# A chain of attention, MoE and routed MoE on one core: low parts earlier in VectorE's queue, two low halves later, one pair of routing dots per step

## Chip, cores and metric

One core of a Trainium2 chip. The metric is the device time of one execution in microseconds. Names used below: TensorE (PE in rows, PEld for its weight loads), VectorE (DVE), ScalarE (ACT), GpSimd (POOL), SyncE (SP), which issues the transfers.

## What is computed

Three parts in a chain, all in float32 (sizes: 8 sequences of 3072 tokens, 256 columns; z has 64).

```python
scores = (1.0 / S) * np.matmul(z, z.transpose(0, 2, 1))
x = u * np.matmul(np.maximum(scores, 0.0) ** 2, v)          # attention
h = x @ w_in                                                # MoE-1, 256 -> 2048
x = (h * (1.0 / (1.0 + np.exp(-h)))) @ w_out
e_idx = np.argmax(x @ w_gate, axis=1)                       # routed MoE-2, 8 experts
for e in range(E):
    mask = e_idx == e
    h = np.maximum(x[mask] @ w1[e], 0.0)
    out[mask] = gate_w[mask, None] * eom[mask, e, None] * (h @ w2[e])
```

## The kernel before

**Splitting.** A float32 product is made of three products of a narrower type: every operand is split into a high part (ScalarE's copy to fp32r, now and then VectorE's CAST at L296) and a low part, what the high part leaves, which is a subtraction on VectorE (L269 in attention, L355 in MoE-1, L690 in MoE-2). TensorE computes high x high, high x low, low x high.

**Items and steps.** The program is one list of items, each with a front and a back. An attention item is one tile of 128 keys against 512 queries: its front makes the scores (two matmuls, L288 and L289, then ReLU and square on ScalarE), its back the product with v (six matmuls of 512 columns, L312 to L314). Scores are symmetric: a tile whose mirror image has been computed is not computed again, it is fetched from memory (`sym`, L241, four transfers issued by SyncE into a staged tile `raw`) and transposed by VectorE (L249, "flip"). A tile on the diagonal is partly fetched. Such a mirrored step has no score matmuls. A MoE-1 item is 128 of the 2048 hidden columns for a block of 512 tokens: front six matmuls (L346), sigmoid on ScalarE (L348), the product g of the two on VectorE (L350), high part on ScalarE (L353); back twelve matmuls of 256 columns (L380 to L382). MoE-2 items are alike.

There are 48 blocks of 512 tokens. The first five blocks' attention items stand alone in the list (24 each); from there attention and MoE-1 items of earlier blocks alternate, then MoE-1 items alone, then MoE-2. Item i's front is in step i, its low part in step i+1, its back in step i+3 (`LOOK`). The names below give a step its number from 0.

**The order.** A scheduler is not at work: each engine executes its instructions in the order in which the program is written, and the loop at the end of `moe_chain` (L953 on) writes it. In each step: `run_tasks(i, 0.0)` writes the tasks whose due step has come; then the front of item i; then the low part of item i-1 (`rest`); then the back of item i-3; then `run_tasks` again with a budget, which takes tasks that are released but not yet due, in the order of their due steps, until their costs have used the budget up. The budget comes from the item whose back it is: 1.1 for most MoE-1 items, 0.8 for attention items that compute scores, 0 for mirrored ones, 1.4 for MoE-2.

**Tasks.** Loads of z, x, v and mirrored scores go through a ring of four `raw` tiles (`DEPTH`); the task of a tile (`f_prep`) works on it and then issues the load of the tile four places later. For z that work is `prep_hl` (the high half by ScalarE, the low half of the lower 64 rows by VectorE, L170), for x it is `f_x` (L209, L210), for mirrored scores the transpose L249. Routing of a finished MoE-1 block is `route_tasks`: 32 dot products on VectorE (`dot`, L390; four rows of tokens by eight experts), two to a task, here a pair; then `pick` (L423 to L437, small operations on VectorE), then, four steps later, `rank` with two small matmuls and the scattered stores by GpSimd. All are released when the block is done and due at the end of the next block. `later(steps, cost, fn, slack)` puts a task a few steps ahead. At block 46 `snapshot` counts the tokens per expert (a matmul at L397 on the running one-hot counts `ohc` that `pick` updates) and makes the table of tiles for MoE-2.

Of the kernel before, what the change touches and what calls it, by code (L numbers as in the profile page):

```python
# [14 lines left out]
ALU = mybir.AluOpType  # L15
AX = mybir.AxisListType

P = 128
# [6 lines left out]
LEAD = 5  # L25
# [10 lines left out]
def r32(ap):  # L36
    return ap.bitcast(F32)
# [7 lines left out]
def moe_chain(tc, zT, uT, vp, win, wout, w12, wgT, wogT, out):  # L45
    nc = tc.nc
    B, NQ, DZ, _ = zT.shape
# [4 lines left out]
    KT = S // P  # L52
# [17 lines left out]
    with ExitStack() as ctx:  # L70
# [13 lines left out]
        def mk(pool, shape, dt, tag, bufs):  # L84
            uid[0] += 1
            return pool.tile(shape, dt, tag=tag, name=f"{tag}_{uid[0]}", bufs=bufs)

        def psum():
            return mk(pp, [P, TQ], F32, "ps", 4)
# [55 lines left out]
        def task(due, release, cost, fn):  # L145
            tasks.append((due, release, len(tasks), cost, fn))

        items = []
        now = [0]

        def later(steps, cost, fn, slack=2):
            i = now[0] + steps
            bisect.insort(queue, (i + slack, i, len(tasks), cost, fn))
            tasks.append(None)
# [3 lines left out]
        hl = [ap_.tile([P, TQ], F32R, name=f"hl{j}") for j in range(NHL)]  # L158
# [8 lines left out]

        def prep_hl(j, zz):
            nc.scalar.activation(hl[j], zz, AF.Copy)
            nc.vector.tensor_tensor(out=hl[j][DZ:P], in0=zz[DZ:P], in1=r32(hl[j][DZ:P]), op=ALU.subtract)  # L170

        def prep_hh(zz):
            h = mk(ap_, [P, TQ], F32R, "hh", 2)
# [26 lines left out]
        def f_x(n, c):  # L200
            def f(t):
                if c == 0:
                    if n == NBLK - 1:
                        h, l = (mk(cp, [P, ND, TQ], F32R, g, 1) for g in ("xf", "x"))
                    else:
                        h, l = (mk(ap_ if g == "xo" else cp, [P, ND, TQ], F32R, g, 1) for g in (("xo", "x") if n % 2 else ("xh", "xl")))
                    xs[n] = [h[:, i, :] for i in range(ND)], [l[:, i, :] for i in range(ND)]
                h, l = xs[n]
                nc.scalar.activation(h[c], t, AF.Copy)  # L209
                nc.vector.tensor_tensor(out=l[c], in0=t, in1=r32(h[c]), op=ALU.subtract)  # L210
            return f


# [10 lines left out]
        def key_order(b, q):  # L224
            if not any(columns(b, q, k) for k in range(KT)):
                return list(range(KT))
            own = range(q * NS, (q + 1) * NS)
            lead = [k for k in range(KT) if k // NS == q + 1]
            o = lead + [k for k in range(KT) if k not in lead and k not in own]
            for s, k in enumerate(own):  # L230
                o.insert(s * KT // NS, k)
            return o
# [152 lines left out]
        def small(shape, dt, tag, bufs=2):  # L385
            return mk(cp, shape, dt, tag, bufs)

        def dot(a, w, res):
            j = mk(cp, [P, TQ], F32, "junk", 1)[:, 0:D]
            nc.vector.tensor_tensor_reduce(out=j, in0=a, in1=w, scale=1.0, scalar=0.0, op0=ALU.mult, op1=ALU.add, accum_out=res)  # L390

        def bc(ap, shape, axis):
            return ap.unsqueeze(axis).to_broadcast(shape)
# [8 lines left out]
        def route_tasks(n, due, release):  # L402
            st = {}
            sh = [P, NS, E]

            def dots(s, e0, ne):
                def f():
                    if "L" not in st:
                        st["L"] = small(sh, F32, "L")
                    for e in range(e0, e0 + ne):  # L410
                        dot(recs[n][:, s, 0:D], wg[:, e, :], st["L"][:, s, e:e + 1])
                return f

            for s in range(NS):
                for e in range(0, E, 2):
                    task(due, release, 0.72, dots(s, e, 2))

            def pick():
                L = st["L"]
                rec = recs[n]  # L420
                d = rec[:, :, D:D + E]
                m = small([P, NS], F32, "m")
                nc.vector.tensor_reduce(out=m, in_=L, axis=AX.X, op=ALU.max)  # L423
                nc.vector.tensor_tensor(out=d, in0=L, in1=bc(m, sh, 2), op=ALU.subtract)
                cand = small(sh, F32, "cand")
                nc.vector.tensor_scalar(out=cand, in0=d, scalar1=0.0, scalar2=None, op0=ALU.is_ge)
                nc.vector.tensor_tensor(out=cand, in0=cand, in1=bc(em8, sh, 1), op=ALU.mult)
                mn = small([P, NS], F32, "mn")
                nc.vector.tensor_reduce(out=mn, in_=cand, axis=AX.X, op=ALU.min)
                oh = small(sh, BF16, "oh")  # L430
                nc.vector.tensor_tensor(out=oh, in0=bc(em8, sh, 1), in1=bc(mn, sh, 2), op=ALU.is_equal)
                pre = small(sh, BF16, "pre")
                nc.vector.tensor_copy(pre[:, 0, :], ohc)
                for s in range(1, NS):
                    nc.vector.tensor_tensor(out=pre[:, s, :], in0=pre[:, s - 1, :], in1=oh[:, s - 1, :], op=ALU.add)
                nc.vector.tensor_tensor(out=ohc, in0=pre[:, NS - 1, :], in1=oh[:, NS - 1, :], op=ALU.add)
                nc.vector.tensor_scalar(out=rec[:, :, D + E], in0=tid, scalar1=float(n * TQ), scalar2=None, op0=ALU.add)  # L437
                st["oh"], st["pre"] = oh, pre
                later(4, 0.6, rank)

            def rank():
                oh, pre = st["oh"], st["pre"]
                ps = psum()
                r = ps[:, 0:NS * E]
                nc.tensor.matmul(r, tri, oh.rearrange("p s e -> p (s e)"), start=True, stop=False)  # L445
                nc.tensor.matmul(r, ones, pre.rearrange("p s e -> p (s e)"), start=False, stop=True)  # L446
                t = small(sh, F32, "t")
                nc.vector.tensor_tensor(out=t, in0=r.rearrange("p (s e) -> p s e", e=E), in1=bc(ecap, sh, 1), op=ALU.add)
                nc.vector.tensor_tensor(out=t, in0=t, in1=oh, op=ALU.mult)
                sf = small([P, NS], F32, "sf")  # L450
                nc.vector.tensor_reduce(out=sf, in_=t, axis=AX.X, op=ALU.add)
                si = small([P, NS], I32, "si")
                nc.vector.tensor_copy(si, sf)
                rec = recs.pop(n)
                for s in range(NS):
                    nc.gpsimd.indirect_dma_start(  # L456
                        out=scr, out_offset=bass.IndirectOffsetOnAxis(ap=si[:, s:s + 1], axis=0),
                        in_=rec[:, s, :], in_offset=None, bounds_check=E * CAP - 1, oob_is_err=False)

            task(due, release, 1.8, pick)  # L460
# [287 lines left out]
        def att_step(n, k):  # L748
            return at_["a", n, k]
# [23 lines left out]
        def f_hl(j):  # L773
            return lambda t: prep_hl(j, t)
# [9 lines left out]
        for n, (b, q) in enumerate(blocks):  # L784
            if q == 0:
                for j in range(NHL):
                    if n:
                        due = att_step(n - 2, KT // 2 + 2 * j) if j < NQ - 2 else att_step(n - 1, KT // 2) if j < NQ - 1 else att_step(n, KT // 2)
                        rel = max(last_use(n - t, range(j * NS, (j + 1) * NS)) for t in range(1, NQ + 1)) + 1
                    else:  # L790
                        due, rel = max(att_step(n, j * NS) - 2, 0), 0
# [7 lines left out]
            if q == 0:  # L799
                for j in range(KT // 2):  # L800
                    rel = used(n - 1, (2 * j, 2 * j + 1)) + LOOK + 1 if n else 0
                    due = min(att_step(n, key_order(b, q).index(2 * j + s)) for s in range(2)) + (-1 if n else 1)
# [96 lines left out]
        for n in range(NBLK):  # L899
            rel = moe_end[n] + LOOK + 2  # L900
            due = moe_end[n + 1] if n + 1 < NBLK else max(m2_at[min(NA // 4, 8)], rel)
            route_tasks(n, due, rel)
            if n == NSNAP - 1 and NA:
                task(due, rel, 1.5, snapshot)
            if n == NBLK - 1:
                task(due, rel, 3.0, final_tables)
# [44 lines left out]
        credit, low = 0.0, None  # L951
        for i in range(NI + LOOK):
            if i < NI:  # L953
                run_tasks(i, 0.0)
                rest, low = low, items[i].front() if items[i].front else None
                if rest:
                    rest()
            elif low:
                low()
                low = None  # L960
            if i >= LOOK:
                if items[i - LOOK].back:
                    items[i - LOOK].back()
                credit = min(credit, 0.0) + items[i - LOOK].budget
                credit = run_tasks(i, credit)
# [74 lines left out]
```

## Time and profile before

| | |
|---|---|
| time, median of 3 runs | 5225.73 us (5225.36 to 5226.89) |
| the profiled execution | 5230.47 us, of which 5228.7 us are the span of the profile |
| mean granted clock of TensorE | 0.998 |
| busy: PE, PEld, DVE, ACT, POOL | 99%, 86%, 75%, 61%, 8% of the span |
| attention alone (first five blocks) | up to about 245 us |
| attention and MoE-1 mixed | to about 4030 us |
| MoE-1 alone, then MoE-2 | to about 4094 us, then to the end |

How to read it: an engine waits where its next instruction is not ready, and the profile names what ended that wait. TensorE's matmuls are pipelined, so their recorded times overlap (a matmul of 512 columns is recorded with 0.39 us and the next starts 0.23 us later), and a wait shows best at the weight load that comes ahead of the matmul. The durations of VectorE's instructions overlap a little too; starts are compared with starts.

### The profile page before, as it was taken

What the parts mean: (1) busy time and instruction counts of PE and PEld (TensorE: products, weight loads), DVE (VectorE), ACT (ScalarE), POOL (GpSimd) and SP (SyncE); (2) the same over time, 40 slices, a digit from 0 to 9 for tenths busy, and PEclk for the clock granted to TensorE, in tenths of its full rate; (3) what the DMA queues carried; (4) which work ended last, traced back from release to release, by engine and by line L of the source; (5) the groups of instructions that cost most, each with busy time, mean ns of one, the idle gap of its engine ahead of it and who ended that gap; (6) DMA issues with size and microseconds to landing.
All of it is one profiled execution on the core that took longest, in us unless ns stands there. A gap on an engine that the chain in (4) does not pass through costs nothing. (4 is left out here: it accounts for less than half of the span.)

```text
span 5228.7 us, 90753 instructions
## 1 busy us (share of the span) xinstructions
PE 5168.0 (99%) x30038; PEld 4520.4 (86%) x30038; DVE 3920.0 (75%) x9802; ACT 3193.9 (61%) x5852; POOL 421.2 (8%) x459
## 2 busy tenths in 40 slices
PE   8999999999999999999999999999999999999998
PEld 6788888888888888888888888888888899999998
DVE  7877688677876786778767877686778786666697
ACT  7856655665566556655666566556654555555576
POOL 0000000000000000000000000000000121111111
PEclk9999999999999999999999999999999999999999
DMA  3343355335433553345334533453344657665575
GB/s 119 103 110 100 103 106 122 99 96 111 111 97 105 112 113 99 100 104 120 102 98 105 112 118 95 109 113 112 95 112 89 187 157 217 180 177 173 156 248 168
DMA packets 1481887, 647.20 MB, mean 124 GB/s; under 512 B 1283261, under 2 KB 1333182, under 8 KB 1465536
## 3 DMA queue, kind: packets, MB, share of 16 engines
q1 hardware_dynamic: 1462592, 589.40, 43.8%
q0 software_dynamic: 18816, 51.93, 2.7%
q8 instruction: 237, 3.88, 0.3%
q14 instruction: 242, 1.98, 0.1%
HBM read 431.16 MB, written 213.16 MB: 123 GB/s over the span
## 5 line engine op out<-in xcount | busy, mean ns | idle before, releaser
L381 PE MATMUL acc<-woutl,hi 128*128 128x256 f32 x3600 | 998.7, 277 | 0.0
L350 DVE TENSOR_TENSOR t<-ps,t 128x512 f32<-128x512 f32 x768 | 529.7, 690 | 603.4 <-ACT t L348 599.1
L313 PE MATMUL acc<-lo,vh 128*128 128x512 f32 x2304 | 911.9, 396 | 30.2 <-DVE lo L269 29.8
L353 ACT ACTIVATE hi<-t 128x512 fp32r<-128x512 f32 x768 | 485.9, 633 | 712.8 <-DVE t L350 712.8
L314 PE MATMUL acc<-hi,vl 128*128 128x512 f32 x2304 | 910.4, 395 | 0.0
L312 PE MATMUL acc<-hi,vh 128*128 128x512 f32 x2304 | 905.1, 393 | 0.0
L382 PE MATMUL acc<-wouth,lo 128*128 128x256 f32 x3072 | 855.5, 278 | 8.4 <-DVE lo L355 8.2
L269 DVE TENSOR_TENSOR lo<-t,hi 128x512 fp32r<-128x512 f32 x1152 | 776.0, 676 | 114.0 <-ACT hi L294 113.1
L380 PE MATMUL acc<-wouth,hi 128*128 128x256 f32 x3072 | 855.1, 278 | 0.0
L381 PEld LDWEIGHTS acc<-woutl,hi 128*128 128x128 f32 x3600 | 677.1, 188 | 28.6
L390 DVE CUSTOM_DVE_ANT_0 junk<-rec,wg 128x256 f32<-128x256 f32 x1536 | 649.0, 423 | 34.4
L348 ACT ACTIVATE t<-ps 128x512 f32<-128x512 f32 x768 | 454.4, 592 | 300.8 <-PE ps L346 298.4
L380 PEld LDWEIGHTS acc<-wouth,hi 128*128 128x128 f32 x3072 | 577.2, 188 | 23.2
L382 PEld LDWEIGHTS acc<-wouth,lo 128*128 128x128 f32 x3072 | 577.7, 188 | 14.2 <-DVE lo L355 13.4
L313 PEld LDWEIGHTS acc<-lo,vh 128*128 128x128 f32 x2304 | 433.6, 188 | 147.8 <-DVE lo L269 50.5
L282 ACT ACTIVATE hi<-t 128x512 fp32r<-128x512 f32 x440 | 277.6, 631 | 424.8 <-DVE t L249 382.6
L355 DVE TENSOR_TENSOR lo<-t,hi 128x512 fp32r<-128x512 f32 x768 | 518.3, 675 | 7.7
L312 PEld LDWEIGHTS acc<-hi,vh 128*128 128x128 f32 x2304 | 434.1, 188 | 95.8
L314 PEld LDWEIGHTS acc<-hi,vl 128*128 128x128 f32 x2304 | 434.0, 188 | 91.6
L456 POOL DMA_INDIRECT scr<-rec,si x192 | 202.1, 1053 | 3709.5 <-DVE t L249 901.5
L688 ACT ACTIVATE hi<-ps 128x512 fp32r<-128x512 f32 (+1 forms) x488 | 253.9, 520 | 386.1 <-PE ps L685 381.6
L690 DVE SCALAR_TENSOR_TENSOR lo<-ps,hi 128x512 fp32r<-128x512 f32 (+1 forms) x488 | 287.9, 591 | 237.6 <-ACT hi L688 237.3
(449 smaller groups left out, 10553.3 us busy)
## 6 DMA issues: line engine op xcount, KB each, us to landing
raw<-in_w_dram SPq DMA_DIRECT2D x122, 1024.0 KB, 6.9
sym<-t SPq DMA_DIRECT2D x440, 256.0 KB, 2.0
raw<-sym SPq DMA_DIRECT2D x1760, 64.0 KB, 2.4
raw<-in_zT_dram SPq DMA_DIRECT2D x192, 128.0 KB, 2.7
raw<-in_vp_dram SPq DMA_DIRECT2D x96, 256.0 KB, 3.0
xf<-in_uT_dram SPq DMA_DIRECT2D x96, 256.0 KB, 3.2
x<-xf SPq DMA_DIRECT2D x96, 256.0 KB, 2.1
raw<-x SPq DMA_DIRECT2D x96, 256.0 KB, 3.0
```

The costliest lines, as they stand in the source:

```text
L269: nc.vector.tensor_tensor(out=lo, in0=a, in1=r32(hi), op=ALU.subtract)
L312: nc.tensor.matmul(acc[:, c, :], h, hi, start=i == 0, stop=False)
L313: nc.tensor.matmul(acc[:, c, :], h, lo, start=False, stop=False)
L314: nc.tensor.matmul(acc[:, c, :], l, hi, start=False, stop=i == KT - 1)
L348: nc.scalar.activation(sg, ps, AF.Sigmoid)
L350: nc.vector.tensor_tensor(out=g, in0=ps, in1=sg, op=ALU.mult)
L353: nc.scalar.activation(hi, g, AF.Copy)
L355: return lambda: nc.vector.tensor_tensor(out=lo, in0=g, in1=r32(hi), op=ALU.subtract)
L380: nc.tensor.matmul(y[:, s, :], a, wh, start=first and s % per_bank == 0, stop=False, skip_group_check=True)
L381: nc.tensor.matmul(y[:, s, :], a, wl, start=False, stop=False, skip_group_check=True)
L382: nc.tensor.matmul(y[:, s, :], l, wh, start=False, stop=last, skip_group_check=True)
L390: nc.vector.tensor_tensor_reduce(out=j, in0=a, in1=w, scale=1.0, scalar=0.0, op0=ALU.mult, op1=ALU.add, accum_out=res)
```

## The change

1. In the loop, the low part of item i-1 is written before the front of item i instead of after it; the due tasks still come ahead of both. The front's instructions on VectorE (L350 in MoE-1, the CAST L296 in attention) now stand behind the low part.
2. From step 120 (`KT * LEAD`) on, the subtraction of the low half of z (L170) and of the low part of x (L210) isn't written with ScalarE's copy, but queued by `later(1, 0, fn, 1)`: released a step later and due a step after that.
3. The cost of a pair of dots is 1.2 instead of 0.72. The budget of most MoE-1 steps is 1.1, so one pair is taken per such step.

```diff
--- before.py
+++ after.py
@@ -167,7 +167,13 @@
 
         def prep_hl(j, zz):
             nc.scalar.activation(hl[j], zz, AF.Copy)
-            nc.vector.tensor_tensor(out=hl[j][DZ:P], in0=zz[DZ:P], in1=r32(hl[j][DZ:P]), op=ALU.subtract)
+            afterwards(lambda: nc.vector.tensor_tensor(out=hl[j][DZ:P], in0=zz[DZ:P], in1=r32(hl[j][DZ:P]), op=ALU.subtract))
+
+        def afterwards(fn):
+            if now[0] > KT * LEAD:
+                later(1, 0, fn, 1)
+            else:
+                fn()
 
         def prep_hh(zz):
             h = mk(ap_, [P, TQ], F32R, "hh", 2)
@@ -207,7 +213,7 @@
                     xs[n] = [h[:, i, :] for i in range(ND)], [l[:, i, :] for i in range(ND)]
                 h, l = xs[n]
                 nc.scalar.activation(h[c], t, AF.Copy)
-                nc.vector.tensor_tensor(out=l[c], in0=t, in1=r32(h[c]), op=ALU.subtract)
+                afterwards(lambda: nc.vector.tensor_tensor(out=l[c], in0=t, in1=r32(h[c]), op=ALU.subtract))
             return f
 
 
@@ -413,7 +419,7 @@
 
             for s in range(NS):
                 for e in range(0, E, 2):
-                    task(due, release, 0.72, dots(s, e, 2))
+                    task(due, release, 1.2, dots(s, e, 2))
 
             def pick():
                 L = st["L"]
@@ -952,9 +958,9 @@
         for i in range(NI + LOOK):
             if i < NI:
                 run_tasks(i, 0.0)
-                rest, low = low, items[i].front() if items[i].front else None
-                if rest:
-                    rest()
+                if low:
+                    low()
+                low = items[i].front() if items[i].front else None
             elif low:
                 low()
                 low = None
```

In the new file the lines behind L176 are shifted by 6: the low parts are L275 and L361, g is L356, the transpose L255, the x low part L216, the dots L396, the pick L429 to L443, the counts L403 and L405.

No engine gets more or fewer instructions. Where they stand, at two places:

**VectorE around step 644** (names: `lo` low parts, `t` at L350 and L356 the product g, `raw` staged tiles, `hl` z, `xl` x). Before, with the front of step 643 as the third row:

```order
2390 L210 TENSOR_TENSOR xl_15726<-raw_15585,xh_15725 128x512
2391 L170 TENSOR_TENSOR hl_106<-raw_15647,hl_106 64x512
...
2394 L350 TENSOR_TENSOR t_3637_15771<-ps_15762,t_3636_15769 128x512
2395 L355 TENSOR_TENSOR lo_15753<-t_3632_15750,hi_15752 128x512
2396 L249 STREAM_TRANSPOSE t_3640_15783<-raw_15662 128x256
2397 L355 TENSOR_TENSOR lo_15774<-t_3637_15771,hi_15773 128x512
2398 L210 TENSOR_TENSOR xl_15726<-raw_15707,xh_15725 128x512
2399 L249 STREAM_TRANSPOSE t_3646_15812<-raw_15729 128x512
```

With the change, from the same front on:

```order
2371 L356 TENSOR_TENSOR t_3620_15709<-ps_15700,t_3619_15707 128x512
2372 L396 ISA junk_15720,L_14943<-rec_14850,wg 128x256
2373 L396 ISA L_14943 128x1
...
2380 L429 TENSOR_REDUCE m_15728<-L_14943 128x4
...
2389 L443 TENSOR_SCALAR rec_14850<-cf 128x4
2390 L255 STREAM_TRANSPOSE t_3636_15759<-raw_15633 128x256
2391 L361 TENSOR_TENSOR lo_15712<-t_3620_15709,hi_15711 128x512
2392 L255 STREAM_TRANSPOSE t_3642_15787<-raw_15748 128x512
2393 L275 TENSOR_TENSOR lo_15768<-t_3636_15759,hi_15767 128x512
2394 L216 TENSOR_TENSOR xl_15746<-raw_15548,xh_15745 128x512
2395 L170 TENSOR_TENSOR hl_106<-raw_15618,hl_106 64x512
2396 L255 STREAM_TRANSPOSE t_3646_15813<-raw_15754 128x512
```

The low part of step 643 (`lo_15774`, now `lo_15712`) stood behind g, the low part of step 642 and one transpose (step 644's, half a tile); now two pairs of dots (eight rows) and the pick (ten rows) stand between g and that transpose, since the block's routing is due there. The low half of z (L170) and the first low part of x, which stood ahead of g, have moved behind the transposes of steps 644 and 645.

**SyncE's issues at the same place**, with the change:

```order
543 L203 DMA raw_15548<-x_13279 128x512
544 L164 DMA raw_15618<-in_zT_dram 64x512
545 L165 DMA raw_15618<-in_zT_dram 64x512
546 L247 DMA raw_15633<-sym_5_5_15292 32x8x32 x4
547 L203 DMA raw_15656<-x_13279 128x512
548 L247 DMA raw_15748<-sym_2_5_13091 32x16x32 x4
549 L247 DMA raw_15754<-sym_2_5_13091 32x16x32 x4
```

These seven stand in the same order as before. `raw_15618` (z) and `raw_15548`, `raw_15656` (x) are given back only by the subtractions above; `raw_15748` goes into the tile that the transpose of `raw_15633` gives back, and `raw_15754` into that of `raw_15748`, where each is used one step after it is issued.

**VectorE around the counts of step 1904** (`L` the dot products, `ohc` the running counts, `cnt` what the counts' matmul on TensorE gives). Before:

```order
7375 L423 TENSOR_REDUCE m_47777<-L_47227 128x4
...
7383 L436 TENSOR_TENSOR ohc<-pre_47787,oh_47785 128x8
7384 L437 TENSOR_SCALAR rec_47134<-cf 128x4
7385 L350 TENSOR_TENSOR t_11105_47803<-ps_47794,t_11104_47801 128x512
7386 L355 TENSOR_TENSOR lo_47762<-t_11095_47759,hi_47761 128x512
7387 L399 COPY cnt_47823<-ps_47821 128x8
```

With the change:

```order
7361 L361 TENSOR_TENSOR lo_47770<-t_11090_47767,hi_47769 128x512
7362 L356 TENSOR_TENSOR t_11097_47798<-ps_47789,t_11096_47796 128x512
7363 L396 ISA junk_47815,L_47227<-rec_47111,wg 128x256
7364 L396 ISA L_47227 128x1
...
7377 L396 ISA junk_47829,L_47227<-rec_47111,wg 128x256
7378 L396 ISA L_47227 128x1
7379 L429 TENSOR_REDUCE m_47831<-L_47227 128x4
...
7387 L442 TENSOR_TENSOR ohc<-pre_47841,oh_47839 128x8
7388 L443 TENSOR_SCALAR rec_47111<-cf 128x4
7389 L405 COPY cnt_47850<-ps_47848 128x8
```

Between the g of step 1903 (`t_11105`, now `t_11097`) and the copy of the counts stood one low part, with the pick ahead of g; now eight dots (sixteen rows) and the pick stand between them. The counts' matmul on TensorE needs `ohc` and stands behind the back of item 1900 as before.

## Rows read from the trace of the kernel before

**Rows 1.** Page, part 1: busy us, share of the span, instructions.
```profile
PE 5168.0 (99%) x30038; PEld 4520.4 (86%) x30038; DVE 3920.0 (75%) x9802; ACT 3193.9 (61%) x5852; POOL 421.2 (8%) x459
```

**Rows 2.** Waits of the weight loads, whole span: us in total, times, longest.
```profile
PEld acc L313 <- DVE lo L269: 50.5, 52, 4.6
PEld acc L382 <- DVE lo L355: 13.4, 25, 1.8
```

**Rows 3.** The same view, 45 to 329 us.
```profile
PEld acc L313 <- DVE lo L269: 7.8, 15, 1.5
```

**Rows 4.** The same view, 329 to 3110 us.
```profile
PEld acc L313 <- DVE lo L269: 11.1, 13, 1.9
PEld acc L382 <- DVE lo L355: 9.1, 19, 1.2
```

**Rows 5.** The same view, 3110 to 3760 us.
```profile
PEld acc L313 <- DVE lo L269: 19.1, 16, 2.3
PEld acc L382 <- DVE lo L355: 3.0, 4, 1.8
```

**Rows 6.** Waits of VectorE, whole span: us in total, times, longest.
```profile
DVE t L350 <- ACT t L348: 599.1, 498, 3.3
...
DVE hl L170 <- ACT hl L169: 37.6, 38, 4.7
```

**Rows 7.** Waits of VectorE, 3110 to 3760 us.
```profile
DVE t L249 <- DMA raw<-sym: 17.0, 15, 2.1
```

**Rows 8.** Timeline, VectorE, 796 to 806: start us, us, instruction [idle before, releaser].
```profile
798.93 0.69 DVE L350 TENSOR_TENSOR t<-ps,t 128x512 f32<-128x512 f32 x1 [0.60 <-ACT t L348]
799.54 0.68 DVE L355 TENSOR_TENSOR lo<-t,hi 128x512 fp32r<-128x512 f32 x1
```

**Rows 9.** Timeline, TensorE, 801.9 to 803.7 us.
```profile
802.45 0.28 PE L382 MATMUL acc<-wouth,lo 128*128 128x256 f32 x1
```

**Rows 10.** Timeline, VectorE, four dots and what follows, 1294 to 1303 us.
```profile
1294.83 0.41 DVE L390 CUSTOM_DVE_ANT_0 junk<-rec,wg 128x256 f32<-128x256 f32 x1
...
1296.57 0.71 DVE L249 STREAM_TRANSPOSE t<-raw 128x512 f32<-128x512 f32 x1
```

**Rows 11.** Timeline, VectorE, a pick and what follows, 1630 to 1637 us.
```profile
1632.92 0.18 DVE L423 TENSOR_REDUCE m<-L 128x4 f32<-128x32 f32 x1
...
1635.08 0.68 DVE L350 TENSOR_TENSOR t<-ps,t 128x512 f32<-128x512 f32 x1
```

**Rows 12.** Timeline, VectorE, step 643, 1353 to 1366 us.
```profile
1360.45 0.69 DVE L350 TENSOR_TENSOR t<-ps,t 128x512 f32<-128x512 f32 x1 [0.69 <-ACT t L348]
```

**Rows 13.** Timeline, TensorE, steps 646 to 649, 1363 to 1374 us.
```profile
1364.18 0.28 PE L382 MATMUL acc<-wouth,lo 128*128 128x256 f32 x1
...
1369.66 0.39 PE L313 MATMUL acc<-lo,vh 128*128 128x512 f32 x1
...
1371.03 0.39 PE L313 MATMUL acc<-lo,vh 128*128 128x512 f32 x1
```

**Rows 14.** Timeline, SyncE's DMA issues, 1353 to 1371 us.
```profile
1357.75 10.95 SPq L241 DMA_DIRECT2D raw<-sym  x20
```

**Rows 15.** Page, part 6: DMA issues, KB each, median us to landing.
```profile
raw<-sym SPq DMA_DIRECT2D x1760, 64.0 KB, 2.4
```

**Rows 16.** Timeline, TensorE, the counts, 4041 to 4046.5 us.
```profile
4044.88 0.17 PE L397 MATMUL ps<-ohc,ones 128*128 128x8 bf16 x1 [0.65 <-DVE ohc L436]
```

**Rows 17.** Timeline, ScalarE, the sigmoid of step 1903, 4041 to 4045 us.
```profile
4042.94 0.60 ACT L348 ACTIVATE t<-ps 128x512 f32<-128x512 f32 x1
```

**Rows 18.** Timeline, TensorE, step 1922, 4100.4 to 4102.6 us.
```profile
4101.55 0.38 PE L382 MATMUL acc<-wouth,lo 128*128 128x256 f32 x1 [0.71 <-DVE lo L355]
```

**Rows 19.** Timeline, TensorE, after a gap, 3220 to 3227 us.
```profile
3222.23 0.51 PE L313 MATMUL acc<-lo,vh 128*128 128x512 f32 x1 [1.86 <-DVE lo L269]
...
3224.36 0.63 PE L346 MATMUL ps<-xo,winl 128*128 128x512 f32 x1
3224.79 0.63 PE L346 MATMUL ps<-x,winh 128*128 128x512 f32 x1
```

## The prediction

> **What bounds the kernel now.** I read the page first: TensorE is busy for 99% of the span [rows 1], so time can go only where it stands still. Its matmuls overlap in the records, so the next view is the waits of its weight loads, which come ahead of the matmuls: 50.5 us are for attention's low parts (L269) and 13.4 us for MoE-1's (L355) [rows 2]. That is the whole stock the change can draw on: some 64 us, 1.2% of the span. Split by stages, 7.8 us lie between 45 and 329 us [rows 3], 20.2 between 329 and 3110 [rows 4], 22.1 between 3110 and 3760 [rows 5], and what is left of the 50.5, some 12 us, in the first 45 us. The third view is what VectorE itself waits for, because a low part stands in its one queue: 599.1 us for ScalarE's sigmoid ahead of L350, 37.6 us for the high half of z (L169) [rows 6].
>
> **The gains.** The sum is made against the profiled execution, 5230.5 us; it lies 4.7 us above the median of the three runs, and I take that off at the end. No engine gets more or fewer instructions; all is order.
>
> *Low part first.* Today a step's L350 stands ahead of the last step's low part: g starts at 798.93 after 0.60 us of waiting for the sigmoid, and the low part at 799.54 [rows 8]. In the new order the low part passes both, so it is done up to 1.2 us earlier; where VectorE is late throughout, it gains only the 0.61 us. The recorded waits between 329 and 3110 us are 20.2 us in 32 pieces, 0.63 each [rows 4]. Most are no longer than what is gained: I take 17 of 20.2 (bounds 8 and 20.2). Between 45 and 329 us the work ahead is a shorter CAST; 4 of 7.8 (2 to 6) [rows 3]. Between 3110 and 3760 us VectorE's transposes wait 17.0 us for their loads [rows 7]; a low part behind such a transpose is still behind it, so 5 of 22.1 (0 to 10) [rows 5]. In the first 45 us loads end last: 1 (0 to 4).
>
> *Low halves of z and x a step later.* They no longer make VectorE wait about 1 us for ScalarE (37.6 us in 38 pieces for z) [rows 6], which serves the same low parts; it is in the 17 already. Their own deadlines are far. What it costs is buffers: the staged tile (a ring of four) stays held a step longer, which is below.
>
> Gains together: 17 + 4 + 5 + 1 = 27 us.
>
> **The losses.** *Bursts.* The routing work of a block (32 dots in 16 tasks, a pair each, then the pick) is spare work with a due step. At 1.2 a pair instead of 0.72 fewer fit into each step's budget, so a dozen blocks reach the due step unfinished (one did before), and what is due runs in one piece, ahead of the low part. Four dots take 1296.57 - 1294.83 = 1.74 us, or 1.86 with the last result's read [rows 10]; a pick 1635.08 - 1632.92 = 2.16 us [rows 11]; a transpose some 0.63, a low part 0.6.
>
> Steps 379 and 1131 get two pairs, a pick and a transpose ahead of the low part of the step before. At 379, g ends at 799.54 [rows 8]; 1.86 + 2.16 + 0.63 + 0.6 later it is 804.8, and TensorE wants that low part at 802.45 [rows 9]: 2.4 us lost, twice.
>
> *Exposed loads.* Steps 644 and 1396 get the same burst: g starts at 1360.45 [rows 12], so it ends at 1361.06; with 4.0 us of dots and pick, a half transpose of 0.44 and the low part, 1366.1 against 1364.18 [rows 13]: 1.9 us. Behind it the tile for the next transpose goes into the buffer that this transpose gives back at 1365.5, because the z and x tiles hold the others. A load is four issues of 0.55 us (10.95 us for 20) [rows 14] and 2.4 us to land [rows 15]: 3 x 0.55 + 2.4 = 4.1 us. So transpose 645 ends at 1370.2, and the buffer for 646 is only then free: another 4.1, and transpose 646 ends at 1374.9. The low part of 645 stands behind transpose 646 in VectorE's queue: done at 1375.5, wanted at 1369.66 [rows 13] plus the 1.9: 3.9 us lost. The low part of 646, at 1376.7, just meets its matmul (1371.03 + 5.8). So 5.8 us, twice. SyncE's queue stands behind these waiting issues too, but its next load is two steps off.
>
> The Trainium skill ("DMA: Bandwidth & Descriptors", section "Rules for kernel authors") says to issue a transfer early and wait for it late; here the change does the opposite. [...]
>
> *The table of tiles.* At step 1904 a matmul (L397) on TensorE itself waits for the pick. Today it comes at 4044.88 after 0.65 us, so it is wanted at 4044.23 [rows 16]. Now four pairs stand between g and the pick: the sigmoid starts at 4042.94 [rows 17] and g ends by 4044.1; 3.7 us of dots and 2.16 of pick make 4050.0: 5.8 lost, 5.1 more than today.
>
> *Step 1920.* Today eight dots and a pick stand ahead of the last MoE-1 low part, and TensorE waits 0.71 us [rows 18]. Now it is eighteen dots: 10 x 0.465 = 4.65 us more, less 0.6 for the low part that has gone ahead and up to 0.7 for an earlier g: 3.6.
>
> *Runs of mirrored steps.* TensorE takes 1371.03 - 1369.66 = 1.37 us a step there [rows 13]. A transpose whose load waits for the transpose one step before has four steps (5.7 us, with the place of the low part's matmul) for load 4.1, transpose 0.6, high part 0.6, low part 0.6 and what is ahead. Step 909 (pick ahead): 2.6 over. Two steps apart gives 6.9 us: 1633 (pair and pick): 2.6 over; 1873 (pick): 1.5. At 869 (only a z tile ahead): 1.0. Steps 419, 1171 and 1670: 1.3 together. Sum 9.0.
>
> *Clock.* After a gap of 1.86 us the matmuls run 0.43 us apart instead of 0.23 for some eight, the lower of TensorE's two clock levels, 1.2 GHz [rows 19]: about 1.4 us on top of the gap. With four or so long new gaps, 5 us (0 to 12).
>
> Losses: 4.8 + 11.6 + 5.1 + 3.6 + 9.0 + 5 = 39 us. Bounds: 20, if ready work shifts into the gaps and loads land in the shortest times; 65, if all the 25 tiles that are now reloaded within four steps of their release (12 before) come late.
>
> **Sum:** 5230.5 - 27 + 39 = 5242.5, less 4.7: **5238 us**, slower by 0.2%. A measurement of this kernel tells about 0.2% (10.5 us) from no change.
>
> **Rivals.**
> 1. *The bursts stay covered* (faster). A low part is used three steps after its front, and in the stretch of MoE-2 a gap of 5.9 us of dots and pick cost only 0.71 us today [rows 18]. If the low part's earlier place leaves the queue so far ahead that bursts cost under 1 us each, a dozen times, with the loads hidden too, the time is 5225.7 - 27 + 10 = 5209. It is decided at 379: is its low part done by 802.5? Against it: in attention steps the cover is 2.9 us [rows 8, 9], not 6.
> 2. *Gain and loss cancel*: losses at 30 or gains at 36; 5216 to 5236. This is a matter of sizes, and the forecast lies just outside.
> 3. *Loads spread.* Each late load holds SyncE's queue, the loads behind it come late in turn, and the 17.0 us of rows 7 appear in the other stages: 65 of losses, 5264.
> 4. *The new order does nothing for the low parts*, because they wait for ScalarE's high part or a transpose: gains 8, losses 39: 5257.
>
> **Chances.** Forecast (5232 to 5248) 0.36, of which a third is within 0.2%; rival 1 0.20; rival 2 0.20; rival 3 0.13; rival 4 0.11. Faster by over 0.2% (under 5215.3): rival 1 with a little of rival 2, 0.23; within: most of rival 2 and a third of the forecast, 0.29; slower: 0.48. The range of 5206 to 5262 leaves out half of rival 3 and the better part of rival 1's tail, together under 2 in 10; the forecast's own is 5228 to 5250.
>
> **What would show it.** Right: the weight loads' waits for low parts fall to near 5 us between 329 and 3110 apart from a dozen gaps of 2 to 6 us at the named steps; L397's counterpart waits almost 6 us; VectorE shows new waits of its transposes for loads behind 644 and 1396; a few stretches of half clock behind them. Wrong: no gap over 1 us at 379 or 1904 (then rival 1), or transposes that wait for loads in many places (rival 3), or waits for low parts as many and as long as before (rival 4).

## The result, and the profile after

| | before | with the change |
|---|---|---|
| median | 5226.02 us (4 runs, 5225.36 to 5226.89) | 5290.28 us (4 runs, 5284.33 to 5296.31) |
| ratio | | 1.0122, 95% interval 1.011 to 1.0135 |
| span of the profile | 5228.7 us | 5294.5 us |
| granted clock | 0.998 | 0.994 |

The change makes the kernel 64 us slower. The forecast was slower too, but by 12 us, and the time lies outside the widest range that the prediction names (5206 to 5262 us). The page's first part, against [rows 1]:

```profile
PE 5189.5 (98%) x30038; PEld 4534.6 (86%) x30038; DVE 3971.6 (75%) x9802; ACT 3222.1 (61%) x5852; POOL 425.8 (8%) x459
```

Span less TensorE's busy time was 60.7 us and is 105.0: 44 us more of standing still. The other 21.5 us are busy time: as many matmuls, recorded longer, in part at the lower clock and in part in MoE-2, where the cause is open (last section). The weight loads' waits, against [rows 2]:

```profile
PEld ps L352 <- DVE xl L216: 27.4, 13, 4.9
PEld ps L352 <- DVE x L216: 26.5, 13, 3.6
PEld acc L319 <- DVE lo L275: 24.2, 22, 2.5
PEld acc L388 <- DVE lo L361: 21.2, 13, 4.3
```

The waits for low parts have fallen as forecast, from 63.9 us to 45.4, though a dozen bursts were added. What is new stands above them: 53.9 us in 26 waits of L352, the MoE-1 front, for the low part of x (L216). Before, no front waited for x. VectorE's waits, against [rows 6, 7]:

```profile
DVE t L356 <- ACT t L354: 366.7, 546, 3.1
...
DVE t L255 <- DMA raw<-sym: 55.1, 34, 3.7
...
DVE hl L170 <- ACT hl L169: 6.7, 3, 4.8
```

VectorE waits less for the sigmoid (366.7 us for 599.1) and for z (6.7 for 37.6), and longer for its loads of mirrored scores, 55.1 us in the whole span. Before, that was:

```profile
DVE t L249 <- DMA raw<-sym: 17.8, 16, 2.1
```

TensorE at four of the places that the prediction named (step 381 and the front behind it; step 646 and the front behind it, 647; the counts of step 1904; the last MoE-1 item, step 1922), one fence for each:

```profile
791.84 0.38 PE L388 MATMUL acc<-wouth,lo 128*128 128x256 f32 x1 [2.35 <-DVE lo L361]
...
797.12 0.67 PE L352 MATMUL ps<-x,winh 128*128 128x512 f32 x1 [2.52 <-DVE x L216]
```

```profile
1361.38 0.39 PE L388 MATMUL acc<-wouth,lo 128*128 128x256 f32 x1 [1.84 <-DVE lo L361]
...
1366.47 0.50 PE L352 MATMUL ps<-xl,winh 128*128 128x512 f32 x1 [3.22 <-DVE xl L216]
...
1371.20 0.80 PE L352 MATMUL ps<-xl,winh 128*128 128x512 f32 x1 [3.76 <-DVE xl L216]
...
1372.22 0.63 PE L319 MATMUL acc<-lo,vh 128*128 128x512 f32 x1
1372.65 0.63 PE L320 MATMUL acc<-hi,vl 128*128 128x512 f32 x1
```

```profile
4097.38 0.17 PE L403 MATMUL ps<-ohc,ones 128*128 128x8 bf16 x1 [5.90 <-DVE ohc L442]
```

```profile
4156.01 0.58 PE L388 MATMUL acc<-wouth,lo 128*128 128x256 f32 x1 [4.13 <-DVE lo L361]
```

The gaps for low parts and for the counts are those of the sum: 2.35 us for a forecast 2.4, 1.84 for 1.9, 5.90 for 5.8, 4.13 for 4.3 (3.6 and the old 0.71). The gaps at L352 (2.52, 3.22, 3.76) are not in it. VectorE at step 645 and 646:

```profile
1364.53 0.71 DVE L255 STREAM_TRANSPOSE t<-raw 128x512 f32<-128x512 f32 x1 [3.21 <-DMA raw<-sym]
1365.16 0.65 DVE L275 TENSOR_TENSOR lo<-t,hi 128x512 fp32r<-128x512 f32 x1
1365.73 0.68 DVE L216 TENSOR_TENSOR xl<-raw,xh 128x512 fp32r<-128x512 f32 x1
...
1369.26 0.71 DVE L255 STREAM_TRANSPOSE t<-raw 128x512 f32<-128x512 f32 x1 [2.13 <-DMA raw<-sym]
...
1370.47 0.68 DVE L216 TENSOR_TENSOR xl<-raw,xh 128x512 fp32r<-128x512 f32 x1
```

The two exposed loads came as worked out: 3.21 and 2.13 us of waiting, and from the end of the first transpose, where the second row starts, to the start of the second, 1369.26 - 1365.16 = 4.1 us for giving the buffer back, four issues and the landing. The Trainium skill's advice to issue early ("DMA: Bandwidth & Descriptors", section "Rules for kernel authors") is borne out by these two waits. Behind each such transpose stands a low part of x (the third and the last row), and the front that reads it is next on TensorE. After 3.76 us of gap the matmuls start 0.43 us apart (1372.22, 1372.65), the lower clock level, as in [rows 19]. The clock had fallen before that gap, 0.8 us after the one of 3.22 us had ended; in this row of one stretch (us; PE, PEld, DVE, ACT, POOL busy and instructions; granted clock; DMA) the clock is the 0.50:

```profile
1367.31:1374.13 6.82, 3.06 (x8) 2.35 (x8) 3.26 (x6) 2.83 (x5) 0.00 (x0) 0.50 0.80 125
```

It needs no burst. At step 607, where no routing work is left over, the first fence is TensorE, the second VectorE:

```profile
1280.01 0.40 PE L352 MATMUL ps<-xo,winl 128*128 128x512 f32 x1
1282.80 0.50 PE L352 MATMUL ps<-x,winh 128*128 128x512 f32 x1 [2.40 <-DVE x L216]
```

```profile
1280.86 0.71 DVE L255 STREAM_TRANSPOSE t<-raw 128x512 f32<-128x512 f32 x1 [2.67 <-DMA raw<-sym]
1281.50 0.65 DVE L275 TENSOR_TENSOR lo<-t,hi 128x512 fp32r<-128x512 f32 x1
1282.07 0.68 DVE L216 TENSOR_TENSOR x<-raw,xo 128x512 fp32r<-128x512 f32 x1
```

A transpose waits 2.67 us for its load, a low part and that of x follow, and the front stands 2.40 us for x.

### The profile page after: what moved, and what is told of

Read it like the earlier page. It is cut to its first block, busy times and chain, and to the rows that moved or that the text cites. A ratio compares the mean times of both kernels' runs of the same rounds, so it can differ in the third digit from the quotient of the medians.

```text
span 5294.5 us, 90895 instructions
## 1 busy us (share of the span) xinstructions
PE 5189.5 (98%) x30038; PEld 4534.6 (86%) x30038; DVE 3971.6 (75%) x9802; ACT 3222.1 (61%) x5852; POOL 425.8 (8%) x459
## 4 chain that ended last, share of the span: by engine, by line
PE 92%; DVE 3%; DMA 2%; ACT 2%; issue 1%; SPq 1%; DVEq 0%; POOL 0%; ACTq 0%; POOLq 0%
PE ps L352 20%; PE ps L691 10%; PE acc L386 10%; PE acc L388 10%; PE acc L387 10%; PE acc L320 9%; PE acc L319 9%; PE acc L318 9%; PE ps L295 3%; PE ps L294 3%; DMA raw<-sym 1%; SPq L247 1%; DVE lo L275 0%; DVE junk L396 0%; DVE t L356 0%
## 5 line engine op out<-in xcount | busy, mean ns | idle before, releaser
L275 DVE TENSOR_TENSOR lo<-t,hi 128x512 fp32r<-128x512 f32 x1152 | 779.0, 679 | 173.7 <-ACT hi L300 158.0
L388 PE MATMUL acc<-wouth,lo 128*128 128x256 f32 x3072 | 853.5, 278 | 18.6 <-DVE lo L361 18.6
L356 DVE TENSOR_TENSOR t<-ps,t 128x512 f32<-128x512 f32 x768 | 530.0, 690 | 384.4 <-ACT t L354 366.7
L361 DVE TENSOR_TENSOR lo<-t,hi 128x512 fp32r<-128x512 f32 x768 | 528.2, 688 | 237.5 <-ACT hi L359 228.0
L396 DVE CUSTOM_DVE_ANT_0 junk<-rec,wg 128x256 f32<-128x256 f32 x1536 | 646.7, 421 | 27.6
```

Source lines behind the costliest of these rows:

```text
L275: nc.vector.tensor_tensor(out=lo, in0=a, in1=r32(hi), op=ALU.subtract)
L356: nc.vector.tensor_tensor(out=g, in0=ps, in1=sg, op=ALU.mult)
L361: return lambda: nc.vector.tensor_tensor(out=lo, in0=g, in1=r32(hi), op=ALU.subtract)
L388: nc.tensor.matmul(y[:, s, :], l, wh, start=False, stop=last, skip_group_check=True)
```

## Experiments

Three theories were set against each other. *Just in time*: the low part of x is now written in the very step whose front reads it, so whatever stands ahead of it on VectorE lies on TensorE's path. *Bursts*: the due routing work costs the time, the wait for x is only where it shows. *Order*: the low part ahead of the front delays g and with it ScalarE. The expectations call them theories 1, 2 and 3. The runs of the kernel before beside these had medians of 5225.5 to 5226.7 us.

**One part undone.**

`a_x_now`:
```diff
-                afterwards(lambda: nc.vector.tensor_tensor(out=l[c], in0=t, in1=r32(h[c]), op=ALU.subtract))
+                nc.vector.tensor_tensor(out=l[c], in0=t, in1=r32(h[c]), op=ALU.subtract)
```


> The changed kernel with the low part of x written at once again, next to ScalarE's copy (z stays later). Theory 1 (just in time: the delayed low part of x falls due in the very step whose MoE-1 front reads it, so all that stands ahead of it on VectorE lies on TensorE's path): the 54 us of weight-load waits of L352 for L216 go, some of it comes back as waits for low parts behind the same bursts; about 5245 us (5230 to 5258). Theory 2 (the bursts of due routing work cost the time, the wait for x is only where it shows): 5275 or more, the same gaps a step later. Theory 3 (the low part ahead of the front delays g and with it ScalarE): no change, 5285.

5243.12 us (5239.11 to 5244.61), ratio to before 1.0028 (1.0017 to 1.004), as theory 1 had it. 47 us come back with one subtraction (by the medians; no run of the changed kernel came within 39 us of a run of this one): the waits for x are gone, and 18 us of them reappear as waits for low parts (63.5 us instead of 45.4):

```profile
PEld acc L388 <- DVE lo L361: 32.6, 24, 4.3
PEld acc L319 <- DVE lo L275: 30.9, 32, 2.5
```

`a_z_now`: the same edit at L170 instead.

> The changed kernel with the low half of z written at once again (x stays later). Theory 1: z is needed many steps later, so its place costs nothing but buffers; within 8 us of 5290. A rival to it, the held buffers (a staged tile kept a step longer makes transposes wait for their loads): 15 to 30 us are won, and the 55 us that VectorE waits for loads of mirrored scores fall by half.

5283.69 us (5279.06 to 5289.18), ratio 1.0112 (1.0096 to 1.0127). Within the 8 us; the held buffers of z are not the loss. VectorE's waits for mirrored loads fell from 55.1 to 42.5 us and bought little. The runs of the two kernels overlap (5284.33 to 5296.31 us for the change), so the 6.6 us between the medians are not shown to be a gain.

`a_cost072`:
```diff
-                    task(due, release, 1.2, dots(s, e, 2))
+                    task(due, release, 0.72, dots(s, e, 2))
```


> The changed kernel with the cost of a pair of dots back at 0.72, the two other parts kept. Theory 1: the waits for x stay at every block, but short (1 to 2.5 us each, some 25 us in all) since no burst stands ahead; about 5235 to 5250. Theory 2: all the loss goes, some 68 us at the dozen places with bursts, and the gain of the new order shows: 5205 to 5225. Theory 3: 5275 to 5285.

5213.62 us (5206.62 to 5215.27), ratio 0.9972 (0.9961 to 0.9982): faster than before, and in the range of theory 2. But the waits for x did not go, they fell to a third:

```profile
PEld acc L319 <- DVE lo L275: 21.8, 21, 2.5
PEld ps L352 <- DVE x L216: 12.5, 7, 2.4
...
PEld ps L352 <- DVE xl L216: 5.4, 4, 2.7
PEld acc L388 <- DVE lo L361: 4.4, 8, 1.8
```

So neither theory has all of it: 77 us hang on the number 1.2 and 47 on x, out of 64 in all. Each makes the other dearer.

`a_front_first`: the loop of before, the other two parts kept.

> The changed kernel with the front written ahead of the last step's low part again, as before; the later halves and the cost of 1.2 kept. Theories 1 and 2: the gain of the new order is lost (some 24 us of waits for low parts come back), 5305 to 5325. Theory 3: the loss goes, 5230 to 5250.

5311.15 us (5309.14 to 5316.38), ratio 1.0165 (1.0151 to 1.0179). The order theory falls: without the new order it is 21 us worse.

**Parts alone and in pairs.**

`low_z`: low part first, z later; x at once, 0.72 (the edits of `a_x_now` and `a_cost072` on the changed kernel).

> Low part first and the low half of z later, x at once and the pair of dots at 0.72: the two costly parts both undone. Theory 1+2 together (a burst costs by itself, and the x written just in time costs a little everywhere and much behind a burst): the 18 us of waits for x that are left with 0.72 go and few come back elsewhere, 5195 to 5206. Bursts alone (x costs nothing without one): 5210 to 5216.

5199.43 us (5198.36 to 5205.14), ratio 0.9949 (0.9936 to 0.9963). The weight loads' waits in the three stretches of [rows 3 to 5], in that order:

```profile
PEld acc L319 <- DVE lo L275: 2.4, 5, 0.9
PEld acc L388 <- DVE lo L361: 0.5, 1, 0.5
```

```profile
PEld acc L388 <- DVE lo L361: 3.3, 11, 0.4
PEld acc L319 <- DVE lo L275: 3.2, 2, 2.6
```

```profile
PEld acc L319 <- DVE lo L275: 12.3, 12, 2.0
PEld acc L388 <- DVE lo L361: 2.6, 3, 1.8
```

7.8 us became 2.9, 20.2 became 6.5, 22.1 became 14.9.

`b_low_first`, `b_z`, `b_later`, `b_cost12`: the kernel before with one part each: the loop; z later; z and x later; 1.2 for a pair.

> The kernel before with the low part first as its only edit. If the 27 us of gain in the prediction were right, about 5199 (5190 to 5205); if the later halves of z are part of that gain, 5205 to 5215; if the new order does nothing for the low parts, 5220 to 5230. Compared with the run that also has z later it gives what z's place is worth.

5218.02 us (5214.52 to 5220.93), ratio 0.9982 (0.9973 to 0.9991). A third of the forecast gain, between two of the expectations. Between 329 and 3110 us, where the prediction put 17 us, the weight loads' waits for low parts went from 20.2 us to 16.7 alone:

```profile
PEld acc L388 <- DVE lo L361: 11.5, 30, 0.5
PEld acc L319 <- DVE lo L275: 5.2, 10, 1.3
```

The 6.5 us of `low_z` need z's later place too.

> The kernel before with the later low half of z as its only edit. If z's later place is a gain by itself (it was worth 18.6 us beside the low part first): 5205 to 5212. If it only pays together with the low part first: 5220 to 5232. The run with both z and x later and nothing else took 5245.

5218.9 us (5211.93 to 5224.68), ratio 0.9987 (0.9978 to 0.9996). Between the two expectations: 7 us by itself, 18.6 beside the low part first.

> The kernel before with the later halves of z and x as its only edit (front first, 0.72). Just in time: a third of the 43 MoE-1 blocks wait 1 to 2.5 us for x, 5235 to 5245. If x costs only behind bursts: 5222 to 5230.

5245.0 us (5238.23 to 5246.98), ratio 1.0034 (1.0022 to 1.0046). x later loses without any burst and without the new order: 26 us against z alone.

> The kernel before with the cost of 1.2 for a pair of dots as its only edit. Bursts by themselves (priced at 39 us in the prediction, with loads and clock): 5255 to 5270. If the bursts cost only because x is written just in time behind them: 5225 to 5235. If the front first makes them worse: above 5275.

5272.14 us (5271.41 to 5287.44), ratio 1.0096 (1.008 to 1.0111), 2 us above the first expectation. The bursts lose 45 us by themselves, in the old order as in the new (`low_z` to `a_x_now`: 44).

**Deadline or delay, and the number.**

`a_x_early`:
```diff
-                prep(moe_at[n] - 3 + c, ...
+                prep(moe_at[n] - (5 if 1 < n < NBLK - 2 else 3) + c, ...
```


> The changed kernel with the tasks of x due two steps earlier (except for the first two and the last two blocks), all three parts kept, the low part of x still a step or two after its high part. Just in time: the low part of x now stands two steps ahead of the front that reads it, and the waits of L352 for L216 (54 us) go, as with x written at once: 5238 to 5252. If it is the delay itself (the held buffers) and not the deadline that costs: 5275 or more.

5254.74 us (5253.0 to 5255.4), ratio 1.0054 (1.004 to 1.0068). The waits for x fall from 53.9 to 5.6 us:

```profile
PEld acc L388 <- DVE lo L361: 34.0, 18, 4.3
PEld acc L319 <- DVE lo L275: 24.2, 20, 2.7
...
PEld ps L352 <- DVE xl L216: 3.1, 2, 2.8
PEld ps L352 <- DVE x L216: 2.5, 1, 2.5
```

The time is 2.7 us above the first expectation. The earlier task is worth 36 of the 47 us by the medians. It also moves the load of x forward in SyncE's queue, and VectorE's waits for mirrored loads fall from 55.1 to 31.8 us, so deadline and order of loads aren't told apart here. The other 11.6 us are not the delay of x alone: the earlier tasks of x leave less of the budget to the dots, and the bursts grow. At the first burst the gap is 3.80 us, where it was 2.93 with x at once. VectorE there, from the first of the dots behind g and then at the pick, `a_x_now`:

```profile
786.34 0.41 DVE L396 CUSTOM_DVE_ANT_0 junk<-rec,wg 128x256 f32<-128x256 f32 x1
...
788.20 0.19 DVE L429 TENSOR_REDUCE m<-L 128x4 f32<-128x32 f32 x1
...
790.35 0.68 DVE L216 TENSOR_TENSOR x<-raw,xo 128x512 fp32r<-128x512 f32 x1
```

and `a_x_early`:

```profile
789.70 0.42 DVE L396 CUSTOM_DVE_ANT_0 junk<-rec,wg 128x256 f32<-128x256 f32 x1
...
792.50 0.19 DVE L429 TENSOR_REDUCE m<-L 128x4 f32<-128x32 f32 x1
```

Four dots (1.86 us) and the subtraction of x have become six dots (2.80 us) without it.

`a_x_early_072`: the same, and 0.72.

> The changed kernel with 0.72 for a pair of dots and the tasks of x due two steps earlier (not for the first two and last two blocks). Where no burst stands ahead, writing x later cost 14 us (5213.6 against 5199.4). If that is the deadline alone: 5196 to 5204, and the waits for x at L352 are gone but for one at the second block. If it is the held buffers: 5209 to 5217, with waits for x replaced by waits for low parts behind transposes.

5200.84 us (5199.33 to 5201.91), ratio 0.9954 (0.994 to 0.9967). Without bursts the earlier task gives back 12.8 of the 14.2 us that x later cost; the 1.4 us left are within the spread of the runs.

`a_mended`: `a_x_early` with 0.9 for a pair.

> All three parts of the change with two numbers mended: the tasks of x due two steps earlier, and 0.9 instead of 1.2 for a pair of dots, at which one block's pick is left over at its due step instead of a dozen. If deadlines alone made the loss: 5193 to 5206, as the run with z later and x at once. If fewer spare pairs per step cost time of their own: 5210 to 5230.

5204.55 us (5200.72 to 5213.5), ratio 0.9961 (0.9947 to 0.9974). All three parts, with two numbers changed, are 21.5 us faster than before: those two numbers made the loss.

`low_z_c100`, `low_z_c50`: `low_z` with 1.0 and with 0.5 for a pair.

> Low part first, z later, x at once, and 1.0 for a pair of dots; two picks are left over at their due steps, against one at 0.72 and twelve at 1.2. Bursts: two of fourteen places' worth of the 44 us between 0.72 and 1.2 at most, 5197 to 5207. A cost that grows with the number itself (pairs spread over more steps, fewer loads taken ahead): 5215 to 5228.

5215.79 us (5213.02 to 5229.73), ratio 0.9985 (0.9976 to 0.9994): 16 us more than at 0.72, outside the first expectation and in the range of the second, a cost that grows with the number. I had counted picks, but eight pairs are left over too (two at 0.72), and the table of tiles falls due with them: the counts' matmul waits 4.02 us (0.4 at 0.72), the last MoE-1 item 3.19 (0.20). That is 6.6 of the 16 us. Another 6.4 us of new gaps stand at the burst places of steps 379, 644, 1131 and 1396 (1.28, 0.87, 1.28 and 2.97 us), though no pick is left over there.

> Low part first, z later, x at once, and 0.5 for a pair of dots, at which no pick is left over (one at 0.72). The last burst of the kernel before, at step 1920, and the wait for the counts are small: 5194 to 5201 if only what is left over at a due step costs; above 5203 if spare pairs taken earlier push low parts back elsewhere.

5339.29 us (5337.03 to 5340.05), ratio 1.0217 (1.0203 to 1.0231): the slowest of all, with nothing left over.

```profile
PEld acc L388 <- DVE lo L361: 101.5, 132, 2.7
PEld acc L319 <- DVE lo L275: 43.9, 60, 2.5
```

At 0.5 a MoE-1 step takes two or three pairs where it took one or two, and weight loads wait for a low part in 192 places. The number has an edge on either side.

## Why the prediction was wrong

| x and the number for a pair (low part first, z later) | 0.72 | 1.2 |
|---|---|---|
| x at once | 5199.4 | 5243.1 |
| x later, its task two steps earlier | 5200.8 | 5254.7 |
| x later | 5213.6 | 5290.3 |

- **The step that failed** is the sentence on the low halves of z and x: "Their own deadlines are far." For z it holds: later is 18.6 us better beside the low part first, and within the bursts no difference is shown (5290.3 against 5283.7, with runs that overlap). For x it is false, and the code says so: the task of the second tile is due two steps ahead of the MoE-1 block's first front (L811 of the new file, `moe_at[n] - 3 + c`), and `later(1, 0, fn, 1)` moves the subtraction two steps on, to the step of that front. The price was put at nothing but buffers. It is 14.2 us without bursts and 47 with them; a task of x two steps earlier gives back 12.8 (5213.6 - 5200.8) and 35.6 of it (5290.3 - 5254.7). In the profiles the 47 us are 30 us of gaps, 10 at the lower clock and some 11 in MoE-2, which may not be x's (last section). The order rows of step 644 held it: the second low part of x, two rows behind those shown, stands behind the two exposed transposes, and I followed the low parts past them, not x.
- **Gain, 27 us: right in size, and its mechanism only in part.** The version that has the low part first and z later (`low_z`) is 27.3 us faster than the runs of before beside it. By stages, from the waits: 4.9 for a forecast 4, 13.7 for 17, 7.2 for 5. But the sum was reasoned from the low part passing g, and that alone brought 8.7 us, with 3.5 of the 17. That low part first and z later give more together (27.3) than alone (8.7 and 7.2, each against the runs of before beside it) I had not said; a plausible reading, not tested by itself, is that the low half of z waits for ScalarE ahead of the low part (35.7 us of waiting in `b_low_first`).
- **Bursts, 39 us with loads and clock: right in kind; that the size is near is partly luck.** 44 us between `low_z` and `a_x_now`, 45 in the old order. With the change, six gaps came within 0.2 us of the sum (2.35 at 379 and at 1131, 1.84 at 644 and at 1396, the counts, step 1920); at 1633 it was 1.79 for 2.6. With x at once, errors cancel: at 379 and 1131 the gaps are 2.93 us, since the subtraction of x stands in the burst; at 644 and 1396 those of 0.8 us and more come to 3.4 and 2.4 us where 5.8 were forecast; at 909, 1633 and 1873 1.07, 2.00 and 1.06 us for 2.6, 2.6 and 1.5; and two gaps of 1.7 us (955.18 and 2564.32 us) were in no term. The three terms of the mirrored steps are also larger than their own parts give: 2.4, 2.1 and 1.2 us.
- **Exposed loads at 644:** forecast 1.9 and 3.9 us for two low parts. With the change 1.84, then 3.22 and 3.76, both for x: the transposes waited as worked out, but the first to be late was another reader.
- **Clock, 5 us (0 to 12): inside its bounds for the bursts.** The lower level cost 8.7 us more in `a_x_now` than in `low_z`, beside 32 us of gaps, and another 10.1 in the change, beside 30 us of gaps; those 10.1 came with x, which the sum didn't have. (Worked out in the last section; busy time as a whole grew by 11 and 21.6 us, and not all of that is the clock.)
- **Rivals.** The time lies above all four, so none is the account. The first (bursts stay covered) fell at 379, its own test. The third (loads spread) came in part: 55.1 us of waiting for mirrored loads, but 26.4 with x at once. The fourth fell: waits for low parts did shrink, though between 329 and 3110 us mostly with z's place.
- With x at once the forecast of 5238 would have been near the 5243 measured, by the luck told under bursts; the range left no room for a price I had put at nothing.

## What to carry to other kernels

Work that is moved to a later step has a reader, and the question is not whether its deadline is far but what stands ahead of it in its queue on the step that reads it: follow every moved instruction to its consumer, also those that seem free. Two delays on one queue cost more than their sum: x cost 14 us alone and 47 behind bursts (36 if the stretch in MoE-2 is not its doing). A number that spreads work over steps has two edges, work left over at the due step above (1.2), work crowding the steps below (0.5), and only the runs find the good value between.

## What the runs showed of the chip that was not expected

*The lower clock level has a price of its own.* After a gap of 3.76 us the next six matmuls start some 0.43 us apart instead of 0.23. The trace gives the stretches in which half the clock was granted (1.2 of 2.4 GHz). These rows are the sums over all of them, first `low_z`, then the change:

```profile
sum 15.87, PE 6.82 PEld 5.50 DVE 5.72 ACT 6.61 POOL 1.27; mean PE 2.27 PEld 1.83 DVE 1.91 ACT 2.20 POOL 0.42
sum 66.73, PE 44.34 PEld 33.60 DVE 35.24 ACT 24.11 POOL 2.24; mean PE 4.03 PEld 3.05 DVE 3.20 ACT 2.19 POOL 0.20
```

TensorE was busy in them for 6.8 and 44.3 us (24.3 in `a_x_now`, 13.6 before). At the full clock that work takes about half (0.23 us a matmul for 0.43), so the level cost 3.4, 22.2, 12.1 and 6.8 us, estimates from these sums. Between `low_z` and the change that is 18.8 us beside 62.5 us of new gaps (42.5 to 105.0), though the mean granted clock only went from 0.998 to 0.994. One gap does not tell whether the clock falls: it fell within 1 us after a gap of 1.86 us [rows 19], with one of 1.24 us not long before it, and after one of 3.22 us (1366.47 us), but after 2.35 us (791.84 us) the matmuls kept their pace until a second gap, of 2.52 us (797.12 us).

*Busy time holds more than the clock.* It grew by 33.0 us between the two. Some 11 us of that stand in MoE-2, in rows like these, first before, then with the change:

```profile
4400.00:4600.00 200.00, 200.00 (x1305) 182.23 (x1304) 135.61 (x316) 105.94 (x217) 37.82 (x36) 1.00 0.68 193
4400.00:4600.00 200.00, 200.00 (x1283) 180.95 (x1282) 134.78 (x315) 104.87 (x214) 40.21 (x39) 1.00 0.72 201
```

TensorE is busy throughout at the full clock and yet does 1.7% fewer matmuls, over some 700 us between 4150 and 5000 us. None of the other profiles shows that for so long, those with the same loop included. The cause is open, and whether the other three runs of the change had it is not on record; so up to 11 of the 64 us, and of the 47 and 36 us told for x, may belong to this and not to the change.
